# Opening zero matmuls: 64 short and 4 long in fp16 in place of three in fp32

## The chip, the cores and the metric

The kernel runs on one core of a Trainium2 chip. The metric is the device time of one execution in microseconds; where several runs are shown, their median counts.

## What is computed

Eight batches of linear attention with eight heads (576 positions, 64 dimensions), each followed by a root-mean-square normalisation, are joined into 4608 tokens of 512 features. A two-layer feed-forward net with a gated activation follows.

```
kv  = einsum('bhsd,bhse->bhde', k, v)
out = einsum('bhsd,bhde->bhse', q, kv)
rms = sqrt(mean(out * out, axis=-1, keepdims=True) + 1e-06)
x   = (out / rms * g_norm) as [B*S, H*D]          # 4608 x 512
h   = x @ w_in                                    # 512 -> 2048
g   = h * (1.0 / (1.0 + exp(-1.702 * h)))
y   = g @ w_out                                   # 2048 -> 512
```

Inputs and output are fp32 in memory; the kernel works in fp16 with fp32 sums. The zero matmuls that this case is about compute nothing that is used.

## The kernel before

The heads are taken in four pairs (`c` = 0 to 3), so that two heads of 64 dimensions fill 128 partitions. Attention of batch `t+1` is woven into the feed-forward net of batch `t` (`dense`), at places written out by hand (`at1`, `at2`); a ninth round handles the last 64 positions of all batches. The order on each engine is the order of the program, since a manual schedule is in force.

Before the first batch's feed-forward net can start, its attention has to be done alone. This opening is what the change touches:

- SyncE issues the loads of pair 0 of `k`, `q`, `v` into staging tiles (`kf`, `qf`, `vf`, L147). GpSimd issues those of pairs 1 to 3, then the pieces of `w_in` (L168) and `w_out` (L191), through its own DMA queue.
- VectorE clears `ident` (L150), `zeros` (L152, 128x512 fp32) and `kvb[1]` (L153), then `eps_t` and `one_t` (L185, L187). `kvb[1]` is the block-diagonal matrix of the second batch; until that batch is computed it holds only zeros.
- ScalarE casts `qf` to `qraw` (L551). VectorE casts `kf` to `kraw` and `vf` to `vbuf` (L552, L553).
- TensorE runs three fp32 matmuls of `zeros` by `zeros` into a PSUM tile that nobody reads, `idle_ps` (L570). Then it goes through the pairs: `q(c)` transposes q in 12 small steps (L391), `kv(c)` multiplies k by v in 12 small steps (L374), `out(c)` applies the matrix (L257), `sums(c)` adds the squares over a head with a matmul by `ones2` (L337). VectorE copies q back from PSUM (L397) and masks kv into `kvb[0]` (L381).
- `busy(n)` (L560) is a helper that issues `n` fp16 matmuls of `kvb[1]` by itself, 128x512, also into `idle_ps`. It stands in the program after `q(0)`, after `kv(0)` and ahead of the first hidden-layer matmuls.
- ScalarE squares (L277), takes a logarithm (L339, `ln`) and an exponential (L345, `rs`); VectorE multiplies it in (`apply`, L351) and so writes `xT`, the input of the feed-forward net.
- `Hidden.mm` (L436) is the first layer's matmul, `gate` (L445) the activation, `project` (L473) the second layer's matmul. `kv` of the batches from the second on (L225) has 128x128 weights and 64 moving columns.

The order of TensorE's work in the opening is written out in the program. The lines ahead of and behind the changed ones are:

```
    for _ in range(3):
        nc.tensor.matmul(idle_ps, zeros[:, 0:P], zeros, start=True, stop=True)
    a0.q(0)
    busy(2)
    a0.kv(0)
    ...
    busy(2)
    a0.out(0)
    a0.q(1)
    a0.kv(1)
    a0.sums(0)
    a0.out(1)
```

Of the kernel before, what the change touches and what calls it, by code (L numbers as in the profile page):

```python
# [8 lines left out]
F32 = mybir.dt.float32  # L9
# [3 lines left out]
P = 128  # L13
# [3 lines left out]
def kernel(  # L17
# [10 lines left out]
    nc = tc.nc  # L28

    B, H, S, D = q.shape  # L30
# [6 lines left out]
    SM = 512  # L37
# [14 lines left out]
    const = ctx.enter_context(tc.tile_pool(name="const", bufs=1))  # L52
# [14 lines left out]
    kvb = [const.tile([P, NPAIR, P], F16, name=f"kvb{i}") for i in range(2)]  # L67
# [80 lines left out]
    g_row = const.tile([1, D], F32)  # L148
    nc.scalar.dma_start(out=g_row, in_=g_norm.unsqueeze(0))
    nc.vector.memset(ident, 0.0)  # L150
    zeros = const.tile([P, SM], F32)
    nc.vector.memset(zeros, 0.0)  # L152
    nc.vector.memset(kvb[1], 0.0)  # L153
    nc.gpsimd.affine_select(
        out=ident,
# [400 lines left out]
    idle_ps = ps_h.tile([P, SM], F32, name="idle", tag="hT")  # L556

    def busy(n):
        for _ in range(n):
            nc.tensor.matmul(  # L560
                idle_ps,
                kvb[1][:, 0, :],
                kvb[1].rearrange("p c r -> p (c r)"),
                start=True,
                stop=True,
            )


    for _ in range(3):
        nc.tensor.matmul(idle_ps, zeros[:, 0:P], zeros, start=True, stop=True)  # L570
    a0.q(0)
    busy(2)
    a0.kv(0)
# [150 lines left out]
```

## Time and profile before

| what | us |
|---|---|
| median of 5 runs | 286.85 |
| lowest and highest run | 286.65 and 288.93 |
| the profiled execution, its own time | 286.67 |
| its span, from the first to the last instruction | 284.9 |
| TensorE busy with matmuls in the span | 278.9 |
| ScalarE busy | 156.2 |
| VectorE busy | 119.5 |

The profile is of one execution. A line of it names an engine (PE is TensorE's matmuls, PEld its weight loads, DVE VectorE, ACT ScalarE, POOL GpSimd, SP SyncE), a line of the program, an operation, what is written and read, the shapes and a count. "Idle before" is the time in which that engine did nothing ahead of the instruction, and the name behind the arrow is what ended that time. Matmuls overlap, so the time that a group takes is read from the start of one to the start of the next thing on the engine, rather than from the duration of one. A weight load and the matmul that uses it are two instructions on one queue; an fp32 matmul of this kernel shows as two passes, each with its load.

### The profile page before, as it was taken

The page shows a single profiled execution, that of the slowest core. Times are in us where ns is not written, and L with a number is a line of the kernel's source. Part 1 is how long each engine was busy: PE and PEld are TensorE (multiplying, and loading weights), DVE is VectorE, ACT ScalarE, POOL GpSimd, SP SyncE. Part 2 cuts the span into 40 slices and gives each one's busy share as a digit, 9 for nine tenths or more (in the row PEclk, how much of TensorE's full clock was granted, in tenths as well). Part 3 has the DMA queues.
Part 4 walks back from the last instruction along what each step waited for, and adds up shares of the span by engine and source line. Part 5 has one row for each costly group of instructions (what it writes and reads, how often), then busy time and mean ns, then how long its engine had stood idle before and what let it go on. Part 6 is the DMA issues. An engine that isn't in the chain of part 4 may idle for free.

```text
span 284.9 us, 4335 instructions
## 1 busy us (share of the span) xinstructions
PE 278.9 (98%) x1707; PEld 135.1 (47%) x1707; DVE 119.5 (42%) x231; ACT 156.2 (55%) x273; POOL 56.9 (20%) x82
## 2 busy tenths in 40 slices
PE   7999999999999999999999999999999999999995
PEld 2444554455445544554455445544454444444443
DVE  2650566527651757157713862286327400110001
ACT  2697449766565646574458536763666375017400
POOL 8841551111211121112011401140002100000000
PEclk9999999999999999999999999999999999999999
DMA  8999999998589356953797279925401410011022
GB/s 176 199 207 205 206 248 241 203 262 148 124 162 257 57 147 160 247 83 73 224 209 136 38 217 198 185 39 184 83 2 37 123 61 2 0 71 76 2 74 74
DMA packets 54069, 38.76 MB, mean 136 GB/s; under 512 B 31218, under 2 KB 50930, under 8 KB 53922
## 3 DMA queue, kind: packets, MB, share of 16 engines
q0 software_dynamic: 14960, 15.58, 33.2%
q1 hardware_dynamic: 38688, 22.39, 30.1%
q10 hardware_dynamic: 402, 0.52, 0.6%
q8 instruction: 13, 0.21, 0.3%
q14 instruction: 6, 0.05, 0.1%
HBM read 36.73 MB, written 9.44 MB: 162 GB/s over the span
## 4 chain that ended last, share of the span: by engine, by line
PE 96%; ACT 2%; DVE 1%; issue 0%
PE hT L436 43%; PE o L473 42%; PE kvp L225 3%; PE idle L570 2%; PE outR L289 2%; PE oh L505 1%; ACT ln L339 1%; PE ss L337 1%; ACT rs L345 1%; ACT sq L277 1%; PE outT L257 0%; PE idle L560 0%; PE q L414 0%; PE outT L268 0%; DVE xT L351 0%
## 5 line engine op out<-in xcount | busy, mean ns | idle before, releaser
L473 PE MATMUL o<-w_out_sb,gT 128*128 128x512 f16 x560 | 130.7, 379 | 0.0
L445 ACT ACTIVATE gT<-hT 128x512 f16<-128x512 f32 x144 | 84.7, 599 | 76.7 <-PE hT L436 76.4
L436 PE MATMUL hT<-xT,w_in_sb 128*128 128x512 f16 x512 | 116.3, 379 | 0.3 <-DVE xT L351 0.3
L436 PEld LDWEIGHTS <-w_in_sb 128*128 128x128 f16 x576 | 54.5, 98 | 62.9 <-issue 1.0
L473 PEld LDWEIGHTS <-gT 128*128 128x128 f16 x560 | 53.0, 98 | 56.3
L483 DVE COPY osb<-o 128x512 f32<-128x512 f32 x20 | 13.8, 691 | 62.4 <-PE o L473 62.4
L321 POOL TENSOR_TENSOR x<-xr,g_all 128x512 f16<-128x512 f32 x12 | 15.2, 1270 | 71.2 <-DVE xr L314 47.2
L216 DVE COPY kpad<-kraw 64x576 f16<-64x576 f16 x56 | 25.0, 446 | 1.6 <-DMA kraw<-in_k_dram 0.3
L300 DVE TENSOR_REDUCE sum<-sq 128x8 f32<-128x512 f16 x24 | 15.8, 679 | 19.9 <-ACT sq L297 19.9
L238 DVE CAST kvb<-kvp 64x128 f16<-64x128 f32 x28 | 8.1, 288 | 36.5 <-PE kvp L225 36.3
L314 DVE TENSOR_TENSOR xr<-outR,sum 128x512 f32<-128x512 f32 x24 | 15.5, 686 | 11.1 <-ACT sum L311 11.1
L112 POOL DMA_DIRECT2D kraw<-in_k_dram x16 | 10.0, 626 | 47.2 <-DVE kpad L216 42.7
L112 POOL DMA_DIRECT2D vbuf<-in_v_dram x16 | 9.7, 610 | 34.8 <-PE kvp L225 29.3
L321 DVE TENSOR_TENSOR x<-xr,g_all 128x512 f16<-128x512 f32 x12 | 15.2, 1265 | 0.7
L297 ACT ACTIVATE sq<-outR 128x512 f16<-128x512 f32 x24 | 13.6, 591 | 2.0 <-PE outR L289 1.6
L225 PEld LDWEIGHTS <-kpad 128*128 128x128 f16 x252 | 11.1, 98 | 6.5 <-DVE kpad L216 0.2
L436 PE MATMUL hT<-x_rem,w_in_sb 128*128 128x512 f16 x64 | 14.0, 379 | 0.0
L277 ACT ACTIVATE sq<-outT 128x512 f16<-128x512 f32 (+1 forms) x16 | 7.7, 481 | 11.2 <-PE outT L257 9.8
L483 ACT COPY osb<-o 128x512 f32<-128x512 f32 x15 | 8.7, 581 | 6.3 <-PE o L473 6.3
L225 PE MATMUL kvp<-vbuf,kpad 128*128 128x64 f16 x252 | 11.9, 193 | 0.0
L310 ACT ACTIVATE sum<-sum,eps_t 128x16 f32<-128x16 f32 x12 | 3.7, 308 | 15.0 <-DVE sum L300 14.9
L339 ACT ACTIVATE ln<-ss,eps_t 128x512 f32<-128x512 f32 (+1 forms) x16 | 9.4, 586 | 3.1 <-PE ss L337 3.1
(65 smaller groups left out, 141.0 us busy)
## 6 DMA issues: line engine op xcount, KB each, us to landing
qf<-in_q_dram SPq DMA_DIRECT2D x5, 1024.0 KB, 8.5
out_dram<-osb SPq DMA_DIRECT2D x10, 512.0 KB, 2.9
kraw<-in_k_dram POOLq DMA_DIRECT2D x12, 288.0 KB, 7.6
vbuf<-in_v_dram POOLq DMA_DIRECT2D x12, 288.0 KB, 5.5
w_out_sb<-in_moe_w_out_dram POOLq DMA_DIRECT2D x3, 512.0 KB, 14.1
out_dram<-osb SPq DMA_DIRECT2D x6, 192.0 KB, 5.4
qf<-in_q_dram POOLq DMA_DIRECT2D x1, 1024.0 KB, 11.8
out_dram<-osb SPq DMA_DIRECT2D x1, 1024.0 KB, 3.8
```

The source lines that it names most:

```text
L112: nc.gpsimd.dma_start(out=raw[n][l * PH : (l + 1) * PH, c0:c1, 0 : NH * D], in_=srcs[n][b].rearrange("(c l) (p j) d -> l p c (j d)", l=2, ...
L216: nc.vector.tensor_copy(out=kpad[r, c, :, l * D : (l + 1) * D], in_=kraw[r, c, 0 : NH * D].rearrange("p (j d) -> p j d", j=NH),)
L225: nc.tensor.matmul(self.kvp[:, c, :], kpad[:, c, j, :], vbuf[:, c, j * D : (j + 1) * D], start=(j == 0), stop=(j == NH - 1),)
L297: nc.scalar.activation(sq, t, AFT.Square)
L300: nc.vector.tensor_reduce(out=self.sum2[:, j % 2, :], in_=sq.rearrange("p (h d) -> p h d", h=H), op=ALU.add, axis=mybir.AxisListType.X,)
L314: nc.vector.tensor_mul(xr[:, i], self.o[j + i].rearrange("p (h d) -> p h d", h=H), s2[:, i, :].unsqueeze(2).to_broadcast([P, H, D]),)
L321: (nc.vector if i else nc.gpsimd).tensor_mul(self.x16[:, j + i, :].rearrange("p (h d) -> p h d", h=H), xr[:, i], g_all.unsqueeze(1).to_bro ...
L339: nc.scalar.activation(ln[:, 0:n], t[:, 0:n], AFT.Ln, bias=eps_t, scale=1.0 / D)
L436: nc.tensor.matmul(self.h[fo], w_in_sb[:, ko, fo * P : (fo + 1) * P], self.x[:, ko], start=(ko == 0), stop=(ko == KO - 1),)
L445: nc.scalar.activation(self.gT[:, fo, :], self.h[fo], AFT.Gelu_apprx_sigmoid)
L473: nc.tensor.matmul(os[mo], gT[:, fo, mo * P : (mo + 1) * P], w_out_sb[:, fo, :], start=(fo == 0), stop=(fo == FO - 1),)
L483: copy(osb[:, mo, :], os[mo])
```

## The change

The tile `zeros` and its memset go. In place of the three fp32 matmuls TensorE gets 64 matmuls in fp16 with the same 128x128 block of `kvb[1]` as weights and 64 moving columns of it, all into the first 64 columns of `idle_ps`, and then, by `busy(4)`, four fp16 matmuls of 128x512. Each of these 68 matmuls has a weight load of its own, so that TensorE's program has 3533 instructions in place of 3398. The first weight load waits for the memset of `kvb[1]`, where the first fp32 matmul waited for the memset of `zeros`. On the other engines no instruction changes place against another, apart from the memset that is gone.

```diff
     nc.vector.memset(ident, 0.0)
-    zeros = const.tile([P, SM], F32)
-    nc.vector.memset(zeros, 0.0)
     nc.vector.memset(kvb[1], 0.0)
...
-    for _ in range(3):
-        nc.tensor.matmul(idle_ps, zeros[:, 0:P], zeros, start=True, stop=True)
+    for _ in range(64):
+        nc.tensor.matmul(
+            idle_ps[:, 0:D], kvb[1][:, 0, :], kvb[1][:, 0, 0:D], start=True, stop=True
+        )
+    busy(4)
     a0.q(0)
     busy(2)
     a0.kv(0)
```

## The prediction

> **What bounds the kernel now.** I read the page first: TensorE is busy nearly all the span, and the chain that ended last runs through it.
>
> ```profile
> span 284.9 us, 4335 instructions
> ...
> PE 278.9 (98%) x1707; PEld 135.1 (47%) x1707; DVE 119.5 (42%) x231; ACT 156.2 (55%) x273; POOL 56.9 (20%) x82
> ...
> PE 96%; ACT 2%; DVE 1%; issue 0%
> ```
>
> So 6.0 us are not covered by matmuls, and the changed lines can only act where some of those lie. The second view was the chain of waits in order of time over the first 24 us (start, length, what).
>
> ```profile
> 1.00 0.50 DVE zeros L152
> ...
> 1.54 5.49 PE idle L570 x6
> 7.02 0.49 PE q L391 x6
> 7.51 0.54 PE idle L560 x2
> 8.05 0.31 PE kv L374 x12
> ...
> 9.36 0.61 ACT sq L277
> ...
> 16.73 0.76 DVE xT L351
> ...
> 17.53 4.48 PE hT L436 x20
> ```
>
> Three stretches follow one another. Up to 9.3 us TensorE sets the pace, and the opening matmuls are most of it. From 9.36 ScalarE does (square, logarithm, exponential of four column groups), up to the last `apply` at 16.73. From 17.53 TensorE runs without a gap worth naming. A gain at the start is therefore worth what is left of it at 17.53. The third view, the timeline of the opening, says what else those steps wait for (start, length, engine, line, idle time before and its releaser).
>
> ```profile
> 5.31 0.83 ACT L551 CAST qraw<-qf 96x768 f16<-96x768 f32 x1 [2.72 <-DMA qf<-in_q_dram]
> 6.88 0.56 DVE L553 CAST vbuf<-vf 96x768 f16<-96x768 f32 x1 [2.00 <-DMA vf<-in_v_dram]
> 6.95 0.42 PEld L391 LDWEIGHTS <-qraw 96*64 96x64 f16 x12 [1.50 <-ACT qraw L551]
> 7.44 0.11 PEld L560 LDWEIGHTS <-kvb 128*128 128x128 f16 x2
> ...
> 9.25 0.31 PEld L391 LDWEIGHTS <-qraw 96*64 96x64 f16 x12 [0.33 <-issue]
> ...
> 12.95 0.38 PE L374 MATMUL kv<-vbuf,kraw 96*64 96x64 f16 x12 [0.21 <-DMA vbuf<-in_v_dram]
> 14.16 0.33 PEld L436 LDWEIGHTS <-w_in_sb 128*128 128x128 f16 x3 [0.33 <-DMA w_in_sb<-in_moe_w_in_dram]
> ```
>
> The data of `q(0)` are cast by 6.14 (5.31 + 0.83), and its transposes start at 6.95: 0.8 us of the opening are matmuls that overran. But at 12.95 `kv(3)` waits for a transfer, and at 14.16 the first hidden-layer matmuls start after another. These two don't move with TensorE.
>
> **The clock.** The record shows full clock from the start. The transposes contradict that: the first twelve take 0.49 us (6.95 to 7.44), the next twelve 0.28 (9.25 to 9.53, where `kv(1)` starts). By 7.45 the two `busy` matmuls stand 0.23 apart, near the 0.22 of the dense stage (4.48 / 20). So TensorE ran at about half speed until some 7.2 us. What raises the rate then is in no row. At the end the record does show a fall, some 2 us after the matmuls stopped at 281.4 (the columns PEclk, DMA share, GB/s come last):
>
> ```profile
> 283.00:284.00 1.00, 0.00 (x0) 0.00 (x0) 0.00 (x0) 0.00 (x0) 0.00 (x0) 0.86 0.26 68
> 284.00:284.90 0.90, 0.00 (x0) 0.00 (x0) 0.00 (x0) 0.00 (x0) 0.00 (x0) 0.50 0.00 0
> ```
>
> **Removed.** The memset of `zeros`, from 1.00 to 1.50 on VectorE. The one of `kvb[1]` (0.27 us) moves up to 1.00, and TensorE, which now waits for that one, can start at 1.00 + 0.27 + 0.05 = 1.32 in place of 1.54: 0.22 earlier. The two small memsets behind it move up too; VectorE then waits for `kf` until 4.15 anyway, so that is worth nothing. No other queue is passed by anything. The three fp32 matmuls go: six passes from 1.54 to 6.95, 5.41 us.
>
> **Added.** 64 pairs of a weight load and a 128x64 fp16 matmul, then 4 pairs with 128x512. The nearest row for the short pair is the same shape in `kv` of the later batches:
>
> ```profile
> 36.05 0.43 PE L225 MATMUL kvp<-vbuf,kpad 128*128 128x64 f16 x9
> 36.32 0.38 PE L473 MATMUL o<-w_out_sb,gT 128*128 128x512 f16 x1
> ```
>
> Nine in 0.27 us: 0.030 each, loads of 128x128 weights included, at full clock. At half clock I take twice that, 0.060: 64 x 0.060 = 3.84. Four long ones at twice 0.22: 1.76. Together 5.60, and 1.32 + 5.60 = 6.92, the same as now. If the rate is set by streamed columns alone, the first transposes give the scale at half clock (six side-by-side pairs of 96 columns in 0.49, so 0.85 ns a column): 4096 + 2048 columns are 5.2 us, and the end is 6.5. If the clock rises early the end could be 1.32 + 64 x 0.030 + 4 x 0.22 = 4.1, and the cast at 6.14 decides. So `q(0)` starts between 6.2 and 6.95; I take 6.6, nearest to the column rate, 0.35 earlier. The added 135 instructions are 4% of TensorE's list, which 13 packets bring in over the whole span (0.3% of the DMA time); I price them at nothing, under the matmuls that run meanwhile, and at one packet of some 1 us if that cover were gone, an estimate from 0.3% of 284.9 us x 16 engines / 13.
>
> A rule speaks against this change. The Trainium skill, TensorE: Matmul & The Clock Gate, Back-to-back issue gap, has a stream of load and matmul pairs take about 81 ns at 128 columns, because the load counts too. By that figure, an estimate, 64 pairs would cost up to 5.2 us at full clock and `q(0)` would start past 8.2; the row above speaks otherwise, and the sum goes by the row.
>
> **What is left of it.** `q(0)` 0.35 earlier means `kv(0)` 0.35 earlier (it needs `vbuf`, cast by 7.44; it would start at 7.70), and the first square at 9.0. ScalarE's chain moves with it until `kv(3)`, which can't start before 12.92. So `out(3)` stays at 13.72 and ends its 0.39 at 14.11; its square can start at 14.13, not 14.29. The sum `ss(3)` stands behind three hidden-layer matmuls that start at 14.16: 14.16 + 3 x 0.22 = 14.82, plus its 0.38, so the last logarithm starts at 15.22, and its row of before has it at 15.34. That leaves 0.12, and I take 0.1. Bounds: 0, if the zero matmuls end at 6.92; 0.55, if neither transfer binds and `kv(0)` starts at 7.50, once `vbuf` is there, in place of 8.05. The profiled execution took 286.67 (span 284.9 and 1.8 around it), so the sum is 286.57; the median of the runs lies 0.18 higher, and on it I forecast 286.75.
>
> **Rivals.** Differences below 0.5% (1.43 us) are about what a measurement of this kernel can't tell from no change.
>
> *The clock comes late, slower.* Its place is the stretch from TensorE's start to 7.2 us, which fp32 passes fill now; it decides if whatever raises the rate counts short matmuls, with loads between them, for less than these passes. Then `busy`, `kv` and `out` up to 9.34 run at half rate: 4 x 0.22 + 0.2 + 0.22 = 1.3 more, less the 0.35: +0.9, 287.7. If half rate lasts to 14 us, each of the stages of 1.64 us has 0.25 + 0.2 + 0.22 + 0.22 = 0.9 us of TensorE to double, part of it beside ScalarE: another 1.0, 288.7. If it lasts into the dense stage, the 20 matmuls from 17.53 double in part: +4, near 291. For it: one of the five runs before took 288.93, so something costs 2 us at times. Against it: matmuls still fill 1.32 to 6.5, 5.2 us in place of 5.41, and `q(0)` follows at once.
>
> The same page, Part 1, has the clock granted after a busy window of about 3.4 us that doesn't start with the kernel, and shows it for a stream of 128-column pairs. That speaks for a grant on time; no run here shows it for 64 columns.
>
> *The loads are not hidden at half clock, slower.* The place is the 64 pairs. A load's row is 98 ns at full clock; in full sight it adds 64 x 0.098 = 6.3, or 5.9 after the 0.35. It decides from 1.8 us in all (28 ns a pair), where the 0.35 is used up and 1.43 passed. Price +1.5 to +5.9. Against it stands the 30 ns row.
>
> *The transfers don't bind.* The whole 0.35 arrives: 286.5.
>
> *Faster.* Nothing in the chain gives over 0.55. It could only come out so if the runs before lose 2 us as the one at 288.93 did and the changed ones don't: near 284.8.
>
> **How the numbers follow.** Forecast 0.52. Late clock 0.30: 0.08 at 287.7, 0.13 at 288.7, 0.09 at 291. Loads in sight 0.09, of it 0.01 under 1.43 us. Transfers free 0.04. Faster 0.05. Same: 0.52 + 0.08 + 0.01 + 0.04 = 0.65; slower 0.13 + 0.09 + 0.08 = 0.30; faster 0.05. The range goes from 286.3 (the 0.55) to 289.5, which leaves out the 291, most of the exposed loads and the 0.05 below: 0.2. The likeliest case alone is 286.3 to 286.9.
>
> **What would show it.** Right: the last long zero matmul ends between 6.3 and 6.9, transposes of `q(0)` at once or at 6.2, the second group of them in 0.28 us, `kv(3)` still waiting for `vbuf` near 12.9, the dense stage from 17.4. Wrong: short pairs over 60 ns apart; two `busy` matmuls 0.43 apart after 7.5 us; a square of group 0 after 9.4; `kv(3)` without a wait.

## The result, and the profile after

The changed kernel is slower: 288.23 us median (286.98 to 289.34, 25 runs) against 286.88 (49 runs of the kernel before); the measured ratio is 1.0038, with a 95% interval of 1.0028 to 1.0048. The runs form two groups, which the clock record of each run tells apart (the granted clock is the share of TensorE's full clock that the chip allows it at a time). In 10 runs the mean granted TensorE clock is 0.998 or more, and their median is 287.20. In 15 runs it is 0.994, and their median is 288.58. The quotient of the medians, 1.0047, is larger than the ratio because the median falls into the upper group. The profiled execution, 288.23 with a span of 286.5, is one of the upper group.

The page of the changed kernel, its span and the chain that ended last:

```profile
span 286.5 us, 4458 instructions
...
PE 93%; DMA 2%; POOL 2%; ACT 0%; DVE 0%; issue 0%
```

A transfer is on the chain now, which was not so before. The chain of waits in order of time (start, length, what) shows where:

```profile
6.60 0.60 POOL kraw L91
7.20 6.19 DMA vbuf<-in_v_dram
13.39 0.14 issue
13.53 0.53 PE kv L372 x12
14.06 0.54 PE ss L335
...
15.48 1.26 PE hT L434 x3
16.74 0.23 PE ss L335
...
18.37 0.76 DVE xT L349
...
19.18 4.48 PE hT L434 x20
```

The zero matmuls are gone from the chain. From 1.85 to 13.4 us it is GpSimd issuing loads and the load of pair 3's `v`. The dense stage starts at 19.18 in place of 17.53, 1.65 us later; the span grew by 1.6. So the whole loss lies ahead of the dense stage. The timeline of that stretch (start, length, engine, line, idle time before and its releaser):

```profile
1.27 3.44 PEld L568 LDWEIGHTS <-kvb 128*128 128x128 f16 x64 [1.27 <-DVE one_t L185]
4.68 1.84 PE L558 MATMUL idle<-kvb 128*128 128x512 f16 x4
6.46 0.45 PE L389 MATMUL q<-ident,qraw 96*64 96x96 f16 x12
8.75 0.60 ACT L275 ACTIVATE sq<-outT 128x512 f16<-128x512 f32 x1 [2.77 <-PE outT L255]
11.68 0.45 PE L389 MATMUL q<-ident,qraw 96*64 96x96 f16 x12
13.53 0.53 PE L372 MATMUL kv<-vbuf,kraw 96*64 96x64 f16 x12 [1.40 <-DMA vbuf<-in_v_dram]
15.28 1.47 PE L434 MATMUL hT<-xT,w_in_sb 128*128 128x512 f16 x3
```

The opening itself went well: 64 pairs from 1.28 to 4.68, 53 ns each, `q(0)` at 6.46 in place of 6.95, the first square at 8.75 in place of 9.36. But `kv(3)` starts at 13.53, 0.58 later than before, behind 1.40 us without work. From there on the matmuls are slow: the first three of the hidden layer take 1.47 us where they took 0.82. The line of before:

```profile
14.17 0.82 PE L436 MATMUL hT<-xT,w_in_sb 128*128 128x512 f16 x3
```

The stages in one-microsecond windows say why. The three columns at the end are PEclk (the granted clock), the DMA share and GB/s; the columns ahead of them are the busy times of PE, PEld, DVE, ACT and POOL. The changed kernel:

```profile
12.00:13.00 1.00, 0.13 (x7) 0.00 (x0) 0.65 (x2) 1.00 (x3) 0.28 (x1) 1.00 1.24 200
13.00:14.00 1.00, 0.47 (x13) 0.44 (x13) 0.00 (x0) 0.14 (x1) 0.54 (x1) 0.59 1.25 205
14.00:15.00 1.00, 1.00 (x6) 0.37 (x4) 0.90 (x2) 0.36 (x1) 1.00 (x2) 0.50 1.32 196
15.00:16.00 1.00, 1.00 (x4) 0.29 (x2) 0.05 (x1) 1.00 (x3) 0.61 (x2) 0.50 1.41 198
16.00:17.00 1.00, 1.00 (x4) 0.36 (x3) 0.64 (x1) 0.33 (x2) 0.59 (x1) 0.71 1.28 210
```

After the idle microsecond the granted clock falls to half at 13.17 and is back at 16.59, 3.41 us later. In the profile before it stays at 1.00 throughout this stretch:

```profile
13.00:14.00 1.00, 0.94 (x15) 0.42 (x15) 0.77 (x3) 1.00 (x3) 0.68 (x1) 1.00 1.22 199
14.00:15.00 1.00, 1.00 (x6) 0.38 (x5) 0.54 (x1) 1.00 (x3) 1.00 (x3) 1.00 1.30 204
```

One more line is new, in the DMA view of the stretch from 9 to 14 us (queue, kind: packets, MB, share of 16 engines):

```profile
q0 software_dynamic: 1240, 0.99, 127.0%
q8 instruction: 1, 0.02, 1.2%
```

Before, the same view has only the first of these queues:

```profile
q0 software_dynamic: 1253, 1.00, 127.1%
```

Queue 8 brings TensorE's instruction list in blocks of 16 KB: in both traces a block comes about every 250 TensorE instructions, 14 over the span now and 13 before. TensorE's records are 124 more (1769 pairs of load and matmul in place of 1707, an fp32 matmul being recorded as two pairs). The text ahead has 135, which the traces do not show. The trace's packet records have the first block at 10.62 us now, 0.95 us long; before, it came at 14.27.

Pair 3's last packet ended at 13.08 in place of 12.54. The loads as a whole were not late: of the last 576 packets of these loads, a third of all and so about pair 3's, 95% had begun by 11.96 us now and by 11.93 before. The last began at 13.00 in place of 12.46, and the last ten follow one another 60 ns apart, in single file. This looks like one DMA engine that is behind the others. That it is the engine which carried the block is inferred, since the trace does not say which engine carried a packet.

### The profile page after: what moved, and what is told of

It reads as the page before. It is cut to its first block, busy times and chain, and to the rows that moved or that the text cites. A ratio compares the mean times of both kernels' runs of the same rounds, so it can differ in the third digit from the quotient of the medians.

```text
span 286.5 us, 4458 instructions
## 1 busy us (share of the span) xinstructions
PE 279.7 (98%) x1769; PEld 137.5 (48%) x1769; DVE 118.7 (41%) x230; ACT 156.2 (55%) x273; POOL 57.3 (20%) x82
## 4 chain that ended last, share of the span: by engine, by line
PE 93%; DMA 2%; POOL 2%; ACT 0%; DVE 0%; issue 0%
PE hT L434 43%; PE o L471 42%; PE kvp L223 3%; DMA vbuf<-in_v_dram 2%; PE outR L287 2%; PE oh L503 1%; PE ss L335 1%; POOL qraw L91 1%; POOL kraw L91 1%; PE outT L255 0%; POOL vbuf L91 0%; PE q L412 0%; PE outT L266 0%; DVE xT L349 0%; ACT ln L337 0%; ACT rs L343 0%
## 6 DMA issues: line engine op xcount, KB each, us to landing
qf<-in_q_dram POOLq DMA_DIRECT2D x1, 1024.0 KB, 11.2
```

## The experiments

Theory A: the added instructions make TensorE ask for its next instruction block earlier. The block then shares a busy DMA engine with pair 3's loads, these land late, `kv(3)` waits, and the gap lets the clock fall. Theory B has two variants: TensorE only runs further ahead of its data, or the short matmuls do the harm themselves. A third theory, C, was that short matmuls don't raise the clock at the start; the trace after already speaks against it (full rate is recorded from 6.35 us).

"Fell" below counts runs whose mean clock is under 0.9965. "Block" is the start of the first instruction block, "kv(3)" that of its matmuls, both in the one profiled execution. Two kernels whose clock came late (e7, e11) are left for the text.

| kernel | runs | fell | median us | of those held | block at us | kv(3) at us |
|---|---|---|---|---|---|---|
| before | 49 | - | 286.88 | - | 14.27 | 12.95 |
| changed | 25 | 15 | 288.23 | 287.20 | 10.62 | 13.53 |
| 12 long (e1) | 12 | 1 | 287.06 | 286.96 | 15.36 | 13.48 |
| 1 fp32, 64 short (e2) | 11 | 6 | 288.42 | 287.41 | 10.62 | 13.47 |
| 2 fp32, 2 long (e3) | 12 | 1 | 286.85 | 286.82 | 14.62 | 13.18 |
| changed, gap filled with 5 (e4) | 12 | 0 | 287.53 | 287.53 | 11.01 | 13.46 |
| 32 short, 8 long (e5) | 12 | 1 | 287.27 | 287.27 | 12.51 | 12.89 |
| 48 short, 6 long (e6) | 12 | 1 | 287.15 | 287.10 | 12.32 | 12.75 |
| before, pair 3 issued later (e8) | 6 | 4 | 289.24 | 287.82 | 14.27 | 14.21 |
| changed, gap filled with 3 (e9) | 12 | 1 | 287.31 | 287.30 | 11.91 | 14.50 |
| 64 short, fewer kv steps (e12) | 5 | 5 | 288.51 | - | 11.17 | 13.67 |
| 24 of 256 columns, cut kv (e13) | 12 | 2 | 287.15 | 287.15 | 12.56 | 13.13 |
| 12 long, idle weight loads (e14) | 9 | 5 | 288.38 | 287.23 | 10.84 | 13.48 |
| 48 of 128 columns (e15) | 12 | 5 | 287.43 | 287.35 | 10.86 | 13.72 |

In the runs of the kernel before that were made beside these, 1 of 112 fell.

**Twelve long matmuls (e1).** The same streamed columns and start, 112 instructions fewer:

```diff
-    for _ in range(64):
-        nc.tensor.matmul(
-            idle_ps[:, 0:D], kvb[1][:, 0, :], kvb[1][:, 0, 0:D], start=True, stop=True
-        )
-    busy(4)
+    busy(12)
```

> 12 fp16 matmuls of 128x512 in place of the 64 short and 4 long ones: the same streamed columns (6144) and the same start, 112 instructions fewer than the changed kernel. Theory A (the added instructions bring a 16 KB block of TensorE's instruction list, seen at 10.6 us after the change and at 14.3 us before it, into the transfers of head pair 3, so that kv(3) waits): the block comes after 13 us, kv(3) starts near 12.9, no fall of the clock, 286.7 to 286.9. Theory B (TensorE only runs ahead of the transfers by 0.5 us more; the instruction count has no part): like the changed kernel, kv(3) at 13.4, the clock falling in about half of the runs, 287.8 to 288.3. Theory C (short matmuls between weight loads count too little for the clock at the start): no fall, TensorE's rate doubles by 7.3 us, 286.7 to 286.9, but the changed kernel should then show a late rise, which its trace doesn't.

287.06, ratio 1.0010 (0.9998 to 1.0021), 1 fall in 12, the block at 15.36. The block is as A has it, and the time lies nearer to A than to B, 0.2 above A's range. `kv(3)` is not as A has it: it started at 13.48 in the profiled execution, with no block near. So pair 3 lands late at times by itself. In this execution the wait was split, 0.42 us ahead of `kv(2)` and 0.71 ahead of `kv(3)`, and the clock held. The lateness is of another kind than in the changed kernel: the whole stream ran behind, with 95% of pair 3's packets begun by 12.16.

**One fp32 and 64 short ones (e2).**

```diff
-    for _ in range(3):
+    for _ in range(1):
         nc.tensor.matmul(idle_ps, zeros[:, 0:P], zeros, start=True, stop=True)
+    for _ in range(64):
+        nc.tensor.matmul(
+            idle_ps[:, 0:D], kvb[1][:, 0, :], kvb[1][:, 0, 0:D], start=True, stop=True
+        )
```

> One fp32 matmul of zeros and then 64 short fp16 ones (nothing long): the late start of before (behind the memset of zeros), the streamed time of before (one third fp32, two thirds short), but 120 instructions more than before. Theory A: the block comes near 11 us, kv(3) starts at 13.4 or later, the time is 287.1 to 287.4 where the clock holds and 288.2 to 288.8 where it falls; median 287.2 to 288.3. Theory B: TensorE starts as late as before, so q(0) at 6.9, kv(3) at 12.9 with little idle time, 286.7 to 286.9.

288.42, ratio 1.0039 (1.0023 to 1.0056), 6 falls in 11, the block at 10.62: A's numbers, the median 0.1 above its range. The start of `q(0)` was misjudged by both theories (6.24, not 6.9, since the rate doubled at 5.3 us in this execution).

**Ahead without more instructions (e3).**

```diff
-    for _ in range(3):
+    for _ in range(2):
         nc.tensor.matmul(idle_ps, zeros[:, 0:P], zeros, start=True, stop=True)
+    busy(2)
```

> Two fp32 matmuls of zeros and two long fp16 ones: as many instructions as before, but TensorE is through with them at about 6.0, so that q(0) starts at the cast of qraw, 6.2 to 6.4, 0.6 ahead of before. Theory A: kv(3) still at 12.9 behind an idle time of 0.7 to 0.9, no or few falls of the clock, 286.6 to 286.8. Theory B: the gap ahead of kv(3) lets the clock fall in about half of the runs, 287.8 to 288.3.

286.85, ratio 0.9998 (0.9986 to 1.0009), 1 fall in 12. `q(0)` started at 6.08 and the lead was gone by `kv(3)`, which began at 13.18 behind 0.67 us of waiting. Running ahead alone neither gains nor loses: B's first variant falls.

**The gap filled (e4, then e9).** Zero matmuls between `q(3)` and `kv(3)` in the changed kernel, five and then three:

```diff
     a0.q(3)
+    busy(5)
     a0.kv(3)
```

> The changed kernel with five more zero matmuls of 128x512 between q(3) and kv(3), where TensorE stood idle for 1.4 us (12.1 to 13.5). If the loss is the clock that falls because of that gap, no run has a clock of 0.994 any more and the time is what the runs with a full clock have, 287.0 to 287.4; the late landing of pair 3 stays (kv(3) at 13.4). If the fall comes from something else, it stays, 288.2.

> The changed kernel with three zero matmuls of 128x512 between q(3) and kv(3) in place of the five of the earlier run. They end before pair 3 has landed. If the gap's falls are what costs 1.4 us: no or few falls, and now 287.1 to 287.3, since the five ran past the landing. If three are too few to hold the clock, falls in some runs, at 288.4 to 288.8.

With five, no fall in 12 runs and 287.53; with three, 1 in 12 and 287.31 (ratio 1.0019 for both; 1.0008 to 1.0030 and 1.0000 to 1.0038). So the gap is what makes the clock fall, and the fall is what costs most. The five ended as `kv(3)` began, at 13.46; pair 3's last packet was through at 12.85. Where `kv(3)` waited for that packet, it began 0.4 to 0.7 us behind its end in the other traces, so this trace does not show whether the five ran past the landing. The timeline of e4:

```profile
12.14 1.25 PE L558 MATMUL idle<-kvb 128*128 128x512 f16 x5
13.46 0.38 PE L372 MATMUL kv<-vbuf,kraw 96*64 96x64 f16 x12
```

With three, 0.4 us of loss stays in the runs whose clock held (287.30 against 286.92 for the runs of before made beside them); in the changed kernel's it was 0.3. The profiled execution of e9 took 288.14 with its clock held: pair 3's last packet ended only at 14.01 and `kv(3)` began at 14.50. So a late landing costs time without a fall too.

**A late landing without any change at TensorE (e8).** Before, with one piece of `w_in` loaded ahead of pair 3:

```diff
     for c in range(1, NPAIR):
+        if c == NPAIR - 1:
+            load_w_in(0, 4, 0, 2)
         for n in "qkv":
             early_load(n, 0, c, c + 1)
-    load_w_in(0, 4, 0, 2)
     load_w_in(0, 4, 2, KO)
```

> Before, with one change in the loads: the first piece of w_in is issued ahead of pair 3's q, k and v, so that pair 3 lands some 1 us later; TensorE's list and its zero matmuls are untouched. If a late landing alone makes TensorE idle ahead of kv(3) and the clock fall, falls come in a third to two thirds of the runs and the time is 287.6 to 288.8, 287.2 to 287.6 in the runs whose clock holds. If the clock falls for what the opening matmuls are, no run falls, and the time is 287.2 to 287.6.

289.24, ratio 1.0068 (1.0044 to 1.0092), 4 falls in 6 runs (289.17 to 290.14), 287.77 and 287.87 in the two whose clock held; all of this is above what was expected. The last packet of pair 3 ended at 13.77 and `kv(3)` began at 14.21. Landing 1.2 us later costs 0.9 us by itself and the clock on top, with the fp32 opening as it was.

**Between 0 and 64 short ones (e5, e6).** 32 short and 8 long, 48 short and 6 long:

```diff
-    for _ in range(64):
+    for _ in range(32):
...
-    busy(4)
+    busy(8)
```

> 32 short and 8 long zero matmuls: the same 6144 streamed columns and the same start, half of the added instructions. Theory A (instruction block ahead of the end of pair 3's transfers): the block comes between 10.6 us (64 short) and 15.4 us (none short), near 13; pair 3 has landed by then, so few falls of the clock (up to 2 in 12) and 286.8 to 287.1. Theory B (short matmuls do the harm themselves, with no part of the block): half of the effect, falls in about 3 or 4 of 12 runs, 287.1 to 287.6.

> 48 short and 6 long zero matmuls, the same 6144 columns. Theory A (the instruction block, at 12.5 us with 32 short ones and at 10.6 with 64, delays whatever transfer TensorE waits for next): the block comes between 11 and 12 us, still ahead of the end of pair 3's transfers (12.5), so falls of the clock again, in a quarter to a half of 12 runs, and 287.2 in the runs whose clock holds. Theory B (each short matmul does some harm): halfway between the 1 of 12 with 32 and the 15 of 25 with 64, about 4 of 12; the block's time then doesn't matter.

One fall in 12 each. With 48, A's expectation missed (the block came at 12.32, not before 12, just as pair 3's last packet ended), and so did B's, which had about 4. Falls do not grow with the number of short matmuls; they jump between 48 and 64, where the block moves ahead of pair 3's end. But the time did not come back whole: 287.27, ratio 1.0016 (1.0007 to 1.0025), with 32. The timeline of that kernel shows what waits next:

```profile
12.89 0.38 PE L372 MATMUL kv<-vbuf,kraw 96*64 96x64 f16 x12 [0.66 <-DMA vbuf<-in_v_dram]
14.80 0.82 PE L434 MATMUL hT<-xT,w_in_sb 128*128 128x512 f16 x3 [0.52 <-DMA w_in_sb<-in_moe_w_in_dram]
```

`kv(3)` is on time, and the hidden layer waits for `w_in` until 14.80 (14.17 before). It does so until 14.88 in e6 and 14.79 in e13, whose blocks came at 12.32 and 12.56. That fits a block which delays whatever is loaded beside it; no run tests it by itself.

**Narrow fp32 matmuls (e7).** 24 of 64 columns in place of 3 of 512:

```diff
-    for _ in range(3):
-        nc.tensor.matmul(idle_ps, zeros[:, 0:P], zeros, start=True, stop=True)
+    for _ in range(24):
+        nc.tensor.matmul(
+            idle_ps[:, 0:D], zeros[:, 0:P], zeros[:, 0:D], start=True, stop=True
+        )
```

> Before's three fp32 matmuls of 512 columns cut into 24 of 64 columns: everything in fp32 and behind the memset of zeros as before, but 84 instructions more. Theory A: the block comes near 11 to 12 us, ahead of the end of pair 3's transfers, falls of the clock in a quarter to a half of the runs, median 287.0 to 288.3. Theory B (short fp16 matmuls are the cause): no falls, 286.7 to 287.0. If the fp32 weight loads are not hidden at 64 columns, q(0) starts later than 6.95, up to 8, and the time is 287 to 287.8 without falls.

294.99, ratio 1.0262 (1.0242 to 1.0281): far outside. The 48 passes took 1.54 to 11.97, 0.22 us each, where 64 columns at the rate of before's passes (0.85 us for 512) would be 0.11. The rest is most likely the fp32 weight loads, not hidden at 64 columns; no run separates them. Full clock is recorded only from 23.36 us on. It tells nothing between A and B.

**Weight loads alone (e11).** Two fp32 matmuls and 120 weight loads of 8 columns:

```diff
-    for _ in range(3):
+    for _ in range(2):
         nc.tensor.matmul(idle_ps, zeros[:, 0:P], zeros, start=True, stop=True)
+    for _ in range(120):
+        nc.tensor.ldweights(kvb[1][:, 0, 0:8])
```

> Before with two fp32 matmuls of zeros in place of three, and then 120 weight loads of 8 columns that no matmul uses: 116 instructions more than before, no short matmul anywhere. If a load takes 15 to 30 ns, q(0) starts at 6.5 to 8. Theory A: the instruction block comes at 10 to 12 us, kv(3) is late (13.2 to 13.5), falls of the clock in a quarter to two thirds of the runs, median 287.1 to 288.6. Theory B (short zero matmuls are the cause): no falls, 286.8 to 287.2 as long as q(0) starts by 7.

289.30, ratio 1.0079 (1.0054 to 1.0103). Inconclusive for A and B, because something else happened: full clock came only at 17.39 us in the profiled execution (289.75). That execution lost 2.9 us, most of it presumably to the late clock. Three of the 6 runs fell besides.

**Fewer instructions behind 64 short ones, and more behind long ones (e12, e13).** e12 leaves out four of the six steps of `kv(0)` to `kv(2)`; e13 cuts these into halves of columns and the long zero matmuls into 256 and 128 columns:

```diff
+            nj = NJ if c == NPAIR - 1 else 2
-            for j in range(NJ):
+            for j in range(nj):
...
-    busy(12)
+    busy(12, 256)
...
-    busy(2)
+    busy(2, 128)
```

> The changed kernel with all its 64 short matmuls, but kv(0), kv(1) and kv(2) do only two of their six steps each (a part of the sum over positions of batch 0 is left out), which takes 48 instructions out of TensorE's list ahead of kv(3), 3485 in all: between the kernel with 32 short ones (3477) and the one with 48 (3505). Theory A: the instruction block comes at 12.2 to 12.6, after most of pair 3, and the clock falls in 0 to 2 of 12 runs; 287.0 to 287.3. Theory B (the short matmuls themselves): falls in about 7 of 12 as in the changed kernel, median 288.2; TensorE has even less to do ahead of kv(3).

> The converse: no matmul of 64 columns among the zero ones (24 of 256 columns open the kernel, the two later pairs are cut into 8 of 128 each), and kv(0) to kv(2) are cut into two halves of columns, so that TensorE's list has 3541 instructions, 8 more than the changed kernel's. Streamed columns are the same. Theory A: the block comes at 10 to 11.5 us, pair 3 lands late, falls in a quarter to two thirds of the runs (fewer than 15 of 25 if the cut kv steps use up TensorE's lead), 287.2 to 288.6. Theory B: falls as rare as with 12 long ones (1 of 12), 286.8 to 287.2.

e12 fell in all 5 runs (288.51), e13 in 2 of 12 (287.15): both against A as it was put, by the length of the whole list. The traces show what was wrong with that. Over the kernels, the block starts 2.5 to 4.5 us after TensorE's 180th instruction, a place picked to fit these traces. In e12 that one comes at 7.95 us, because all 64 pairs still stand ahead of it, and the block came at 11.17; in e13 most added instructions stand behind it, and the block came at 12.56. By the time of the block, both fit. But e12 has in its trace no straggling packets: as in e1, the whole stream was late (95% begun by 12.42). And short matmuls and an early block still went together in every kernel.

**An early block without short matmuls (e14, e15).** e14 puts eight weight loads that nothing uses behind each of the twelve long zero matmuls; e15 opens with 48 matmuls of 128 columns:

```diff
-    busy(12)
+    for _ in range(12):
+        busy(1)
+        for _ in range(8):
+            nc.tensor.ldweights(kvb[1][:, 0, 0:8])
```

> The kernel with 12 long zero matmuls, with eight weight loads of 8 columns that nothing uses behind each: no short matmul, the same streamed columns, 96 instructions more than with 12 long ones alone, all of them ahead of q(0). Over the runs so far the first instruction block started 2.4 to 4.5 us after TensorE's 180th instruction, which is reached at 7.5 us in the changed kernel and at 11.3 with 12 long ones. Theory A: it is reached near 8 here, the block comes at 10.5 to 11.7, ahead of the end of pair 3's transfers, and the clock falls in a third to all of the runs, median 287.2 to 288.6. Theory B (64 short matmuls do the harm, whatever the block): as with 12 long ones, falls in 1 of 12, 286.9 to 287.2. If the loads are not hidden beside the long matmuls, q(0) comes later by up to 2 us and the 180th instruction at 10, which tells nothing between the two.

> 48 zero matmuls of 128 columns open the kernel, the two later pairs of long ones are cut into 8 of 128 each, and kv(0) alone is cut into two halves of columns: the same streamed columns, no zero matmul of 64 columns, and the 180th instruction at 7.6 to 8.0 us. Theory A: the block at 10 to 12 us, falls in a third to all of the runs, median 287.2 to 288.6. Theory B: few falls (1 or 2 of 12), 286.9 to 287.2.

e14: 288.38, ratio 1.0050 (1.0031 to 1.0070), 5 falls in 9, the block at 10.84. `q(0)` started at 6.14, so that the loads cost TensorE nothing. From e1 it differs by these loads alone, and e1 had 287.06 and 1 fall in 12. The DMA view of e14 from 9 to 14 us, and its `kv(3)`:

```profile
q0 software_dynamic: 1238, 0.99, 126.3%
q8 instruction: 1, 0.02, 1.2%
```

```profile
13.48 0.38 PE L372 MATMUL kv<-vbuf,kraw 96*64 96x64 f16 x12 [1.45 <-DMA vbuf<-in_v_dram]
```

The same wait as in the changed kernel, with no short zero matmul in the program. e15: 287.43, ratio 1.0034 (1.0019 to 1.0049), 5 falls in 12, the block at 10.86. Taken together, the unfilled kernels with a block before 11.2 us (changed, e2, e12, e14, e15) fell in 36 of 62 runs, those with a block after 12.3 (e1, e3, e5, e6, e13) in 6 of 60. Theory A holds in this: enough added TensorE instructions early in the list cost the time, short matmuls or not, and the loss goes with an early block. That the block itself holds the packets up is inferred. For it speaks that the last packet of pair 3 began 0.88 to 1.66 us after the 95% mark in the kernels with a block before 12 us (changed, e2, e4, e9, e14, e15), with e12 (0.47) as the exception, and 0.38 to 0.76 in all others.

## Why the prediction was wrong

- **Removed, and the price of the added work: right.** TensorE started at 1.28 (1.32 forecast). A short pair took 53 ns at half rate; the row of 30 ns at full clock, doubled, gave 60, and the column rate gave 54. `q(0)` came at 6.46 (6.6 forecast). The Trainium skill, TensorE: Matmul & The Clock Gate, Back-to-back issue gap, has 128-column pairs take about 81 ns. The 64-column pairs don't test that; e15's 128-column pairs do, and they stood 56 ns apart at full clock (7.94 to 8.39 for eight).
- **"I price them at nothing, under the matmuls that run meanwhile": the step that failed.** The text looked for the cost of the added instructions at TensorE, which had plenty to do. The bound that it gave, one packet of some 1 us, was the right size (0.95 us). The cover was the wrong one: it counted on matmuls, but the packet came among pair 3's loads, which TensorE waits for. Pair 3's last packet ended 0.54 later, `kv(3)` began 0.58 later, and the gap took the clock. An opening of long matmuls with 96 extra loads hidden beside them (e14) has the whole loss, 288.38, where the same without them (e1) has 287.06.
- **"These two don't move with TensorE": wrong.** That `kv(3)` waits for its transfer was read correctly. But the landing was taken for a fixed 12.9. It moved to 13.5 in the changed kernel, and e1 shows that it can move without a block too. Where the clock held, the sum should have been +0.3, not -0.1.
- **The clock: the rival was right in kind and wrong in place.** It priced a clock that comes late. The clock came on time (6.35 us), and was taken away again at 13.17 for 3.41 us, since TensorE's lead and the late landing together left 1.4 us of idle time. The rival's price for half rate from 9.3 to 14 us, another 1.0 us, is not far from the 1.4 measured between the two groups, for 3.41 us at half rate. e11 shows the case that it named, at +2.9; in e7 (+8.1) the clock came late too, but its opening also ran 5 us over.
- **The loads hidden: right** at half rate for fp16; e7 suggests that it does not carry over to fp32 at 64 columns.
- **"Faster": did not occur.** The lead of 0.6 us at the first square was lost by `kv(3)`, and e3 shows a like lead without extra instructions to be worth nothing (ratio 0.9998).
- **The range and the signs: luck.** 288.23 lies inside 286.3 to 289.5, but the upper part of that range stood for a clock that comes late. None of the signs named for "wrong" came: short pairs 53 ns apart, the first square at 8.75, `kv(3)` behind a wait. What failed had no sign. And a difference of 0.4%, which the text counted as too small to tell from none, is told by these runs (1.0028 to 1.0048).

What stays open: why pair 3's whole stream ran behind in e1 and e12, so that `kv(3)` began as late in e1 (13.48) as in the changed kernel with no block near, and yet only 1 run of e1 in 12 fell. One profile for each kernel does not tell how often that is so.

## What to carry to other kernels

Count the instructions as well as their time: a longer list brings the next instruction block earlier, and if that falls among loads that an engine waits for, they can land later (here by 0.54 us). Where a wait for data is just covered, making the engine ahead of it faster only widens the wait, and on TensorE a gap of some 1.4 us among small matmuls can cost the clock for 3.41 us more. If such a gap can't be closed, a few long dummy matmuls in it hold the clock (no fall in 12 runs with five, one with three).

## What the runs showed of the hardware

- The clock changes on a grid of 3.41 us that stands differently to the kernel's start in each execution: full rate was granted at 6.35 us, taken at 13.17 (two steps later) and granted at 16.59 in the changed kernel; before, it was granted at 7.24 and taken at 283.72, 81 steps later. The Trainium skill, TensorE: Matmul & The Clock Gate, Part 1, gives that window as about 3.4 us and free-running; the traces agree.
- A step does not have to be idle to cost the clock. The one that ended at 13.17 had TensorE busy for 2.09 of 3.41 us, but only three matmuls of 128x512 in it. In e12 a step with four of them was followed by a fall. Steps with five (before, 10.65 to 14.07) and seven (e2, 12.14 to 15.55, with 2.00 us busy and the same idle time in it) were not. So the busy share alone does not decide. Whether it is the number of long matmuls that counts was not tried.
- Eight weight loads of 8 columns that no matmul uses cost TensorE nothing beside each long matmul: `q(0)` began at 6.14 in e14 and at 6.08 in e1. Where such loads stood alone behind two fp32 matmuls, full clock came only at 17.39 us (e11), and behind narrow fp32 matmuls only at 23.36 (e7).
